# Nine transposed chunks of attention weights, moved through PSUM in three pieces of three instead of five and four

## The chip, the cores and the metric

The kernel runs on one core of a Trainium2 chip. The metric is the device time of one execution in microseconds, lower is better, and the number that is compared is the median of several executions.

## What is computed

A sparse attention, then two mixing blocks. All of it is float32.

```
q, k, v: (4 batches, 8 heads, 576 tokens, 64)
scores = q @ k^T / 8
mask   = scores >= 32nd largest score of the row
attn   = softmax of the scores under the mask          # 576 x 576 per head
x      = attn @ v, heads side by side                  # (4, 576, 512)

block 1: theta = x @ w_theta; zr, zi = x cos(theta), x sin(theta)
         u = x + w_tok_r @ zr + w_tok_i @ zi;  x = u + relu(u @ w_ch)
block 2: h = relu(x @ w_in), halves u and v; v normalised over its 512 channels
         out = (u * (w_spatial @ v + b_spatial)) @ w_out
```

## The kernel before

**The attention.** Two heads of a batch make a visit: 16 visits, each of nine tiles of 128 query rows by 576 keys (`NT = 9`; the ninth tile holds the last 64 rows of both heads). That makes 144 tiles, taken two at a time (`G = 2`): 72 pairs. What happens to a pair, function by function:

- `scores(n)`: four float32r matmuls into the PSUM tile `ps_s` (L449), and a copy by ScalarE (ACT) into the SBUF tile `x` (L453), for one tile of the pair.
- `topk(g)`: VectorE (DVE) finds the 32nd largest score of every row of both tiles. Max and min windows (L468, L469), MAX8 and MATCH_REPLACE8 (L472, L478, L481), then three small coefficients `cf` (L489 to L491, partly on ACT).
- `weigh(n)`: ACT makes a sign from the threshold (L500) and the exponential (L501), GpSimd (POOL) multiplies them into `sg` (the helper at L89, two pieces of 288 columns to a tile). `sg` holds both tiles of the pair side by side: 1152 columns of unnormalised weights, which is nine chunks of 128.
- `transpose(n)`: TensorE (PE) transposes the chunks into the PSUM tile `ps_t` (L511), and one ACT instruction copies them to the SBUF tile `ptb` (L512, a Relu, which also turns the negative products of masked keys to zero). The even tile's call takes chunks 0 to 4, the odd one's chunks 5 to 8. There is one `ps_t` of five chunks, 2560 bytes of each partition, which reaches over two banks. There are two `ptb`.
- `values(n)`: once for the pair, 9 to 20 matmuls of the transposed chunks with the values of `v` into `ps_v` (L522, L533, L536). Chunk 4, the one that holds the last columns of the even tile and the first of the odd one, goes first when both tiles have one row block each.

PSUM is full: `ps_s` has two banks, `ps_t` two, `ps_v` one, and `ps_m`, the rotating output of the mixing blocks, three.

**The mixing blocks.** They are generators (`block`, `front`, `middle`, `last`) that yield an estimated cost after each PSUM tile. Each product of two float32 operands is three float32r matmuls (`mm3`, L572 to L574). `advance(quota)` pulls them forward between the attention's steps, a fixed quota of estimated nanoseconds at a time. Batch b's blocks can begin when all of batch b's heads are done, so the first batch's attention (18 pairs) has next to no matrix work beside it, and the last batch's blocks run after the attention's end.

**What sets the order.** Every engine runs its instructions in a fixed order. A planner lays that order down when the kernel is built, out of priorities (`tc.high_priority`), of its own estimate of times, and of when buffers come free. `at(f, n)` calls a step under a raised priority. The calls of one pair stand in the loop as: `weigh` of both tiles, then for each tile `scores` of a later tile, `advance`, `transpose`, `advance`, and `values` at the end.

**Weights that are loaded early.** In the last batch, weights of three products go into attention buffers as these come free (`EXTRA`, `load_extra`): the last two chunks of the low half of `w_spatial` go into the two `ptb`.

Of the kernel before, what the change touches and what calls it, by code (L numbers as in the profile page):

```python
# [10 lines left out]
F32 = mybir.dt.float32  # L11
F32R = mybir.dt.float32r
I32 = mybir.dt.int32
AF = mybir.ActivationFunctionType
# [10 lines left out]
def sparse_attention_then_moe_kernel(  # L25
# [26 lines left out]
    G = 2  # L52
# [15 lines left out]
    att = ctx.enter_context(tc.tile_pool(name="att", bufs=2))  # L68
# [4 lines left out]
    psum = ctx.enter_context(tc.tile_pool(name="psum", bufs=1, space=bass.MemoryType.PSUM))  # L73

    act, dve, pe = nc.scalar, nc.vector, nc.tensor
# [21 lines left out]
    ident = const.tile([128, 128], F32, name="ident")  # L97
# [22 lines left out]
    for i in range(2):  # L120
        chunks = const.tile([128, 4, 3, D + 1], F32, name=f"vc{i}")
# [127 lines left out]
    def split_rest(exact):  # L249
# [9 lines left out]
        (B - 1, "ti"): [(f"{n}{s}", 2, 1) for n in ("q2", "k2") for s in range(2) for _ in range(2)],  # L259
        (B - 1, "ch"): [("x", 3, 2), ("x", 3, 2), ("sg", 2, 2), ("sg", 2, 2)],  # L260
        (B - 1, "sp"): [("kl0", 2, 1), ("kl0", 2, 1), ("kl1", 2, 1), ("kl1", 2, 1), ("raw", 2, 1), ("raw", 2, 1),
                        ("ptb", 2, 1), ("ptb", 2, 1)],
    }

    class Weights:
# [70 lines left out]
    def run(exact):  # L336
# [96 lines left out]
        X, SG, MX, PT = {}, {}, {}, {}  # L433
# [68 lines left out]
            pool.tensor_tensor(sg, x, sg, op=OP.mult)  # L502

        def transpose(n):
            x = SG[n // G].rearrange("p i n -> p (i n)")
            pt = psum.tile([128, 5, 128], F32, name="ps_t")
            ptb = att.tile([128, 5, 128], F32, name="ptb", bufs=2)
            k = (5, 4)[n % G]
            for c in range(k):
                lo = (c + 5 * (n % G)) * 128  # L510
                pe.transpose(pt[:, c, :], x[:, lo:lo + 128], ident)  # L511
            act.activation(ptb[:, 0:k], pt[:, 0:k], AF.Relu)  # L512
            PT[n] = ptb

        def values(n):

            pair = tiles[n - 1:n + 1]
            av = psum.tile([128, 3, D + 1], F32, name="ps_v")
            alone = any(t == 8 for _, _, _, t in pair)
            both = PT[n - 1][:, 4]  # L520
            if not alone:
                pe.matmul(av[:, 0:2], both, vaug[pair[0][0] % 2][1], start=True, stop=False)  # L522
            col = 0
            for i, (visit, b, j, t) in enumerate(pair):
                chunks, mixed, extra = vaug[visit % 2]
                pt = PT.pop(n - 1 + i)
                end = half[i]
                for s in range(2) if t == 8 else (t % 2,):
                    slot = 2 * s if t == 8 else s
                    q = half[s] if t == 8 else slice(0, 128)  # L530
                    o = av[0:64 if t == 8 else 128, col]
                    for c in range(4):
                        pe.matmul(o, pt[:, c, q], chunks[:, c, slot], start=alone and c == 0,  # L533
                                  stop=not alone and i == 1 and c == 3)
                    if alone:
                        pe.matmul(o, both[end, q], extra[end] if t == 8 and s == 1 else mixed[end, i], start=False,  # L536
                                  stop=True)
                    col += 1
            at = 0
            for i, (visit, b, j, t) in enumerate(pair):  # L540
                if t == 8:
                    act.activation(xr[0:64, 4], av[0:64, at:at + 2], AF.Copy)
                    at += 2
                elif alone or i == 0:
                    k = 1 if alone else 2
                    act.activation(xr.rearrange("p i s d -> p (i s) d")[:, t:t + k], av[:, at:at + k], AF.Copy)
                    at += 1

                if t == 8:
                    normalise(b, j, 3 if visit == NP - 1 else 0, 5)  # L550
                elif visit == NP - 1 and t % 2 and t < 7:
                    normalise(b, j, t // 2, t // 2 + 1)
# [3 lines left out]
        def normalise(b, j, lo, hi):  # L556
            if lo == 0:
                XN[b, j] = big.tile([128, 5, 2, D], F32, name="xn", bufs=6)
            xn = XN[b, j]
            i = slice(lo, hi)  # L560
            rs = tmp.tile([128, 5, 2], F32, name="rs")
            dve.tensor_scalar(rs[:, i], xr[:, i, :, D], 1e-9, None, op0=OP.add)
            dve.reciprocal(rs[:, i], rs[:, i])
            pool.tensor_tensor(xn[:, i], xr[:, i, :, 0:D], rs[:, i, :, None].to_broadcast([128, hi - lo, 2, D]),
                               op=OP.mult)
            if hi == 5:
                pool.tensor_tensor(xn[64:128, 4], xr[0:64, 4, :, 0:D],
                                   rs[0:64, 4, :, None].to_broadcast([64, 2, D]), op=OP.mult)
# [450 lines left out]
        for g in range(N // G + 2):  # L1019
            with tc.high_priority(offset=AHEAD):  # L1020
                if g < N // G:
                    topk(g)
                    with tc.issue_after(GATE[g]):
                        if g:
                            next(conv, None)
                        if g == SPLIT:
                            for _ in conv:
                                pass
            n0 = G * g
            for i in range(G):  # L1030
                step(n0 + i)
                at(weigh, n0 - G + i)
            q = FIRST_QUOTA if n0 < PER else QUOTA
            for i in range(G):
                at(scores, n0 + G + 1 + i)
                advance(q)
                at(transpose, n0 - G + i)
                advance(q)
                if i == G - 1:
                    at(values, n0 - G + i)  # L1040
# [52 lines left out]
```

## Time and profile before

| what | value |
| --- | --- |
| median of 3 executions | 989.75 us (989.65 to 991.41) |
| the profiled execution, its own time | 992.02 us |
| its span, first to last instruction | 990.2 us |
| PE busy | 867.8 us (88%) |
| PE weight loads (PEld) busy, beside PE | 797.5 us (81%) |
| DVE busy | 823.0 us (83%) |
| ACT busy | 638.0 us (64%) |
| POOL busy | 598.7 us (60%) |

The attention's last matmul starts at 838.0 us; the rest of the span is the last batch's mixing blocks. Busy times are sums over the span, which has stages with different limits, so a share of the whole says little about one stage. An idle time stands in front of an instruction, together with what ended it.

### The profile page before, as it was taken

The page shows a single profiled execution, that of the slowest core. Times are in us where ns is not written, and L with a number is a line of the kernel's source. Part 1 is how long each engine was busy: PE and PEld are TensorE (multiplying, and loading weights), DVE is VectorE, ACT ScalarE, POOL GpSimd, SP SyncE. Part 2 cuts the span into 40 slices and gives each one's busy share as a digit, 9 for nine tenths or more (in the row PEclk, how much of TensorE's full clock was granted, in tenths as well). Part 3 has the DMA queues.
Part 4 walks back from the last instruction along what each step waited for, and adds up shares of the span by engine and source line. Part 5 has one row for each costly group of instructions (what it writes and reads, how often), then busy time and mean ns, then how long its engine had stood idle before and what let it go on. Part 6 is the DMA issues. An engine that isn't in the chain of part 4 may idle for free.

```text
span 990.2 us, 18081 instructions
## 1 busy us (share of the span) xinstructions
PE 867.8 (88%) x5802; PEld 797.5 (81%) x5802; DVE 823.0 (83%) x2710; ACT 638.0 (64%) x1319; POOL 598.7 (60%) x753
## 2 busy tenths in 40 slices
PE   4657686678779799989999999999989999999997
PEld 2546575667669798888889998898889998889987
DVE  6999999999998897889999998999998981363552
ACT  5566676779858566877776777777966775350121
POOL 2798876686956755594767666676584564421030
PEclk9955556679779699999999999899999999999999
DMA  7797665545817633744362753552743554441221
GB/s 218 215 305 227 215 210 179 145 145 186 261 60 199 230 95 106 229 143 126 110 206 60 229 160 78 218 129 95 205 160 91 201 188 166 191 168 62 104 85 52
DMA packets 79395, 159.78 MB, mean 161 GB/s; under 512 B 36143, under 2 KB 40239, under 8 KB 71866
## 3 DMA queue, kind: packets, MB, share of 16 engines
q1 hardware_dynamic: 79290, 158.53, 50.5%
q8 instruction: 48, 0.79, 0.3%
q14 instruction: 57, 0.47, 0.2%
HBM read 108.63 MB, written 23.32 MB: 133 GB/s over the span
## 4 chain that ended last, share of the span: by engine, by line
PE 43%; DVE 26%; ACT 10%; DMA 9%; POOL 6%; issue 4%; SPq 2%; ACTq 0%; POOLq 0%; DVEq 0%
PE ps_m L574 9%; PE ps_m L572 9%; PE ps_m L573 9%; PE ps_v L533 7%; DVE mm L469 4%; PE ps_s L449 4%; PE ps_t L511 4%; DVE mm L481 4%; DVE mx L478 4%; DVE z L472 2%; DVE mm L468 2%; DMA raw<-in_q_dram 2%; DMA q<-hi 2%; ACT sg L500 1%; POOL sg L89 1%
## 5 line engine op out<-in xcount | busy, mean ns | idle before, releaser
L89 POOL TENSOR_TENSOR sg<-x,sg 128x288 f32<-128x288 f32 x288 | 238.5, 857 | 141.0 <-ACT x L501 94.2
L511 PE MATMUL ps_t<-ident,sg 128*128 128x128 f32 x648 | 140.9, 314 | 60.7 <-POOL sg L89 37.5
L533 PE MATMUL ps_v<-vc,ptb 128*128 128x65 f32 (+1 forms) x1280 | 183.5, 281 | 4.7 <-ACT ptb L512 4.7
L533 PEld LDWEIGHTS ps_v<-vc,ptb 128*128 128x128 f32 (+1 forms) x1280 | 174.7, 206 | 13.6 <-ACT ptb L512 6.7
L511 PEld LDWEIGHTS ps_t<-ident,sg 128*128 128x128 f32 x648 | 97.8, 171 | 77.6 <-POOL sg L89 51.2
L500 ACT ACTIVATE sg<-x,cf 128x576 f32<-128x576 f32 x144 | 103.8, 768 | 44.2 <-DVE cf L491 43.3
L478 DVE MAX8 mx<-mm 128x8 f32<-128x160 f32 x432 | 118.8, 312 | 0.0
L453 ACT ACTIVATE x<-ps_s 128x576 f32<-128x576 f32 x144 | 92.6, 643 | 35.9 <-PE ps_s L449 32.3
L512 ACT ACTIVATE ptb<-ps_t 128x640 f32<-128x640 f32 (+1 forms) x144 | 92.7, 644 | 29.8 <-PE ps_t L511 28.2
L501 ACT ACTIVATE x<-x,cf 128x576 f32<-128x576 f32 x144 | 107.9, 767 | 0.1
L449 PE MATMUL ps_s<-k,q 128*128 128x288 f32 x256 | 91.3, 368 | 16.2 <-DVE q L369 8.6
L572 PE MATMUL ps_m<-w_t,zah 128*128 128x288 f32 (+2 forms) x272 | 98.9, 364 | 6.6 <-DVE F L588 4.8
L574 PE MATMUL ps_m<-w_t,zal 128*128 128x288 f32 (+2 forms) x272 | 97.5, 360 | 0.6 <-POOL zal L89 0.5
L573 PE MATMUL ps_m<-w_t,zah 128*128 128x288 f32 (+2 forms) x272 | 96.7, 356 | 0.0
L472 DVE MAX8 z<-mm 128x8 f32<-128x312 f32 (+1 forms) x288 | 89.6, 372 | 2.0
L572 PE MATMUL ps_m<-w_t,zbh 128*128 128x288 f32 x288 | 85.7, 302 | 2.3 <-DMA w_t<-d_sph 1.0
L481 DVE MATCH_REPLACE8 mm<-mx,mm 128x160 f32<-128x160 f32 x288 | 86.8, 308 | 0.0
L573 PE MATMUL ps_m<-w_t,zbh 128*128 128x288 f32 x288 | 86.2, 303 | 0.0
L574 PE MATMUL ps_m<-w_t,zbl 128*128 128x288 f32 x288 | 84.9, 302 | 1.2 <-POOL zbl L89 1.2
L449 PE MATMUL ps_s<-kl,q 128*128 128x288 f32 x256 | 82.9, 334 | 0.0
L468 DVE TENSOR_TENSOR mm<-x 128x576 f32<-128x576 f32 x72 | 67.7, 941 | 17.5 <-ACT x L453 16.4
L89 POOL TENSOR_TENSOR raw<-raw,hi 128x288 fp32r<-128x288 f32 x60 | 56.2, 956 | 40.2 <-ACT hi L393 40.0
(174 smaller groups left out, 2438.9 us busy)
## 6 DMA issues: line engine op xcount, KB each, us to landing
k<-hi SPq DMA_DIRECT2D x60, 144.0 KB, 2.5
kl<-raw SPq DMA_DIRECT2D x60, 144.0 KB, 2.6
vc<-in_v_dram SPq DMA_DIRECT2D x48, 128.0 KB, 2.9
w_t<-d_trh SPq DMA_DIRECT2D x4, 1152.0 KB
w_t<-d_trl SPq DMA_DIRECT2D x4, 1152.0 KB
out_dram<-t SPq DMA_DIRECT2D x32, 144.0 KB, 2.5
raw<-in_q_dram SPq DMA_DIRECT2D x15, 288.0 KB, 3.0
q<-hi SPq DMA_DIRECT2D x30, 144.0 KB, 3.3
```

The costliest lines, as they stand in the source:

```text
L89: nc.gpsimd.tensor_tensor(out[:, lo:hi], a[:, lo:hi], b[:, lo:hi], op=op)
L449: pe.matmul(o, q, k[:, m], start=a == 0, stop=a == len(terms) - 1)
L472: dve.max(out=z[:, i, QUARTER + 8 * k:QUARTER + 8 * k + 8], in_=mm[:, i, losers])
L478: last = dve.max(out=top[i], in_=src[i])
L481: dve.match_replace(out=mr[i], in_to_replace=top[i], in_values=src[i], imm_value=NEG)
L500: act.activation(sg, x, AF.Sign, bias=cf[:, 2:3])
L501: act.activation(x, x, AF.Exp, bias=cf[:, 0:1], scale=0.125)
L511: pe.transpose(pt[:, c, :], x[:, lo:lo + 128], ident)
L533: pe.matmul(o, pt[:, c, q], chunks[:, c, slot], start=alone and c == 0, stop=not alone and i == 1 and c == 3)
L572: pe.matmul(out, ah, bh, start=first, stop=False)
L573: pe.matmul(out, ah, bl, start=False, stop=False)
L574: pe.matmul(out, al, bh, start=False, stop=last)
```

## The change

The nine chunks of a pair are taken in three pieces of three. Each piece has a PSUM tile of its own out of two (1536 bytes of each partition, so one bank each, two banks as before) and one of three `ptb`. The even tile's call takes piece 0 (chunks 0 to 2), the odd one's pieces 1 and 2. `values` reads chunks by their number out of a list. The two early loads into `ptb` become one, of both chunks, into the buffer `mm` of the top-k step.

```diff
@@ EXTRA
-                        ("ptb", 2, 1), ("ptb", 2, 1)],
+                        ("mm", 1, 2)],
@@ transpose
             x = SG[n // G].rearrange("p i n -> p (i n)")
-            pt = psum.tile([128, 5, 128], F32, name="ps_t")
-            ptb = att.tile([128, 5, 128], F32, name="ptb", bufs=2)
-            k = (5, 4)[n % G]
-            for c in range(k):
-                lo = (c + 5 * (n % G)) * 128
-                pe.transpose(pt[:, c, :], x[:, lo:lo + 128], ident)
-            act.activation(ptb[:, 0:k], pt[:, 0:k], AF.Relu)
-            PT[n] = ptb
+            for part in ((0,), (1, 2))[n % G]:
+                pt = psum.tile([128, 3, 128], F32, name="ps_t", bufs=2)
+                ptb = att.tile([128, 3, 128], F32, name="ptb", bufs=3)
+                for c in range(3):
+                    lo = (c + 3 * part) * 128
+                    pe.transpose(pt[:, c, :], x[:, lo:lo + 128], ident)
+                act.activation(ptb, pt, AF.Relu)
+                PT.setdefault(n // G, []).extend(ptb[:, c] for c in range(3))
@@ values
-            both = PT[n - 1][:, 4]
+            pts = PT.pop(n // G)
+            both = pts[4]
...
-                pt = PT.pop(n - 1 + i)
...
-                        pe.matmul(o, pt[:, c, q], chunks[:, c, slot], start=alone and c == 0,
+                        pe.matmul(o, pts[5 * i + c][:, q], chunks[:, c, slot], start=alone and c == 0,
```

## Rows read from the trace of the kernel before

**Rows 1.** The page's chain that ended last, by engine.
```profile
PE 43%; DVE 26%; ACT 10%; DMA 9%; POOL 6%; issue 4%; SPq 2%; ACTq 0%; POOLq 0%; DVEq 0%
```
**Rows 2.** Windows: stretch, length; busy us (count) of PE, PEld, DVE, ACT, POOL; PE clock; DMA.
```profile
50.00:250.00 200.00, 147.13 (x730) 125.24 (x731) 196.02 (x597) 145.94 (x294) 153.01 (x170) 0.63 0.64 201
250.00:350.00 100.00, 82.34 (x528) 76.33 (x527) 91.06 (x269) 67.78 (x142) 71.50 (x88) 0.82 0.58 182
350.00:838.00 488.00, 468.97 (x3467) 439.38 (x3465) 429.63 (x1554) 357.00 (x754) 313.40 (x397) 0.99 0.48 150
838.00:990.20 152.20, 143.20 (x981) 135.33 (x981) 65.36 (x157) 39.47 (x80) 37.36 (x47) 0.99 0.31 114
```
**Rows 3.** Waits of PE from 50 to 250 us: total, times, longest.
```profile
PE ps_t L511 <- POOL sg L89: 27.7, 15, 6.4
PE ps_t L511 <- ACT ptb L512: 9.6, 5, 3.7
PE ps_v L522 <- ACT ptb L512: 8.4, 7, 3.3
```
**Rows 4.** Waits of PE from 250 to 838 us.
```profile
PE ps_t L511 <- ACT ptb L512: 12.1, 6, 5.5
PE ps_t L511 <- POOL sg L89: 7.2, 8, 2.2
PE ps_s L449 <- ACT x L453: 2.7, 5, 1.4
```
**Rows 5.** Waits of PE from 350 to 838 us.
```profile
PE ps_t L511 <- ACT ptb L512: 4.4, 4, 2.4
PE ps_t L511 <- POOL sg L89: 2.6, 3, 1.7
```
**Rows 6.** Groups of instructions by form: busy us, mean ns, idle before and releasers.
```profile
L511 PE MATMUL ps_t<-ident,sg 128*128 128x128 f32 x648 | 140.9, 314 | 60.7 <-POOL sg L89 37.5 <-ACT ptb L512 21.6 <-POOL vt L588 1.2
L512 ACT ACTIVATE ptb<-ps_t 128x640 f32<-128x640 f32 x72 | 50.1, 696 | 13.0 <-PE ps_t L511 11.7 <-PE ps_v L533 1.0
L512 ACT ACTIVATE ptb<-ps_t 128x512 f32<-128x512 f32 x72 | 42.6, 591 | 16.8 <-PE ps_t L511 16.5
```
**Rows 7.** Timeline, PE from 200 to 260 us: start, length, instruction, [idle before].
```profile
213.12 0.61 PE L511 MATMUL ps_t<-ident,sg 128*128 128x128 f32 x4
217.20 0.47 PE L511 MATMUL ps_t<-ident,sg 128*128 128x128 f32 x1 [3.00 <-POOL sg L89]
218.46 0.80 PE L522 MATMUL ps_v<-vm,ptb 128*128 128x130 f32 x2 [0.79 <-ACT ptb L512]
```
**Rows 8.** Timeline, all engines, 281 to 297 us.
```profile
286.29 0.15 DVE L491 SCALAR_TENSOR_TENSOR cf<-cf,mx 128x2 f32<-128x2 f32 x1
286.48 1.44 ACT L500 ACTIVATE sg<-x,cf 128x576 f32<-128x576 f32 x2 [3.86 <-DVE cf L491]
287.83 0.68 ACT L512 ACTIVATE ptb<-ps_t 128x640 f32<-128x640 f32 x1
...
288.56 1.11 PE L511 MATMUL ps_t<-ident,sg 128*128 128x128 f32 x4 [5.48 <-ACT ptb L512]
...
296.03 0.65 ACT L453 ACTIVATE x<-ps_s 128x576 f32<-128x576 f32 x1 [5.07 <-PE ps_s L449]
```
**Rows 9.** Windows of 10 us, columns as in rows 2.
```profile
280.00:290.00 10.00, 4.52 (x32) 4.29 (x32) 9.90 (x24) 4.81 (x10) 6.45 (x9) 0.76 0.27 74
290.00:300.00 10.00, 10.00 (x62) 10.00 (x62) 7.49 (x28) 4.61 (x12) 3.99 (x6) 0.73 0.25 71
...
340.00:350.00 10.00, 10.00 (x72) 10.00 (x70) 9.90 (x35) 3.92 (x10) 3.25 (x4) 0.84 0.01 2
```
**Rows 10.** SP's queue around the attention's end, and the first PE wait afterwards.
```profile
838.02 0.80 SPq L284 DMA_DIRECT2D w_t<-d_spl  x2
840.04 0.32 SPq L284 DMA_DIRECT2D w_t<-d_thh  x1
840.48 0.35 SPq L284 DMA_DIRECT2D w_t<-d_thl  x1
```
**Rows 11.** Instructions on tile mm, 780 to 860 us: the last use of mm.
```profile
L478 DVE MAX8 mx<-mm x18: 261/314/322, 786.0 to 807.6; 128x8 f32<-128x160 f32 x18
```

## The prediction

> **What bounds the kernel now.** I read the chain of waits first, then busy times by stretch, then PE's waits by stretch. The chain is shared: 43% PE, 26% DVE, 10% ACT [rows 1], so no single engine's total gives the answer. The windows sort it into stages [rows 2]. From 50 to 250 us DVE is busy 196.0 of 200 us and PE 147.1, much of it at the lower clock (mean 0.63): the top-k step sets the pace and PE has 53 us to spare. From 350 to 838 us it is the other way: PE is busy 469.0 of 488 us at clock 0.99 and DVE 429.6, so a wait of PE there is worth up to its length. From 250 to 350 us both are short of full (PE 82.3, DVE 91.1 of 100): the mixing blocks begin, and each engine at times waits for the other. From 838 us on, 152.2 us, there is no attention, so the change has nothing to act on but a weight load. I therefore count what the change does to PE from 250 to 838 us, and nearly nothing of what it does before 250 us.
>
> Where do the transposes wait? PE's idle time before L511 is 60.7 us, of it 21.6 us for the copy out of `ps_t` and 37.5 us for POOL's product `sg` [rows 6]. The stages divide that unevenly. From 50 to 250 us it is 9.6 us for the copy and 27.7 us for POOL, and another 8.4 us in which `values` waits for a copy [rows 3]. From 250 to 838 us it is 12.1 us in 6 waits for the copy and 7.2 us for POOL [rows 4], of which 4.4 us in 4 waits and 2.6 us fall after 350 us [rows 5]. So 12.1 - 4.4 = 7.7 us in two waits lie between 250 and 350 us.
>
> The longer one can be read line by line [rows 8]. The second four transposes wait 5.48 us for the 640-column copy that must empty the only `ps_t`. That copy is itself late: ACT works in order, and ahead of the copy stand the two signs of the next pair, which waited 3.86 us for DVE's `cf`. When PE is through, it runs slowly: the granted clock is 0.73 on average in the following 10 us with PE busy throughout [rows 9]. The wait also reaches DVE: ACT's copy of the next scores had waited 5.07 us for PE [rows 8], and DVE, at 9.90 of 10 us before, falls to 7.49 [rows 9].
>
> **The change part by part.**
>
> *Transposes on PE.* 648 of the same size before and after, 9 to a pair. Cost 0.
>
> *Copies on ACT.* The two forms give the price: (696 - 591) / 128 columns = 0.82 ns a column, so 384 columns cost 591 - 128 x 0.82 = 486 ns [rows 6]. That form is not in the trace, so this is an estimate by a straight line. Three of them are 1458 ns against 696 + 591 = 1287: 171 ns more to a pair, 12.3 us more of ACT over 72 pairs. ACT is busy 357 of 488 us from 350 to 838 us [rows 2]; its spare quarter covers this, save where PE is waiting for ACT at that moment. From 250 to 838 us these are the 6 waits for the copy and 5 for ACT's copy of the scores [rows 4], so between 0 and 11 x 0.17 = 1.9 us. I take the middle, +1.0. Without that cover the whole 12.3 us would count, which is a rival below.
>
> *Two PSUM tiles instead of one.* The wait of the second transposes for the first copy goes. What is late next is the third piece, which needs the first piece's copy gone. Had that copy been stuck behind the signs as at 287.83 us [rows 8], PE would get three more transposes done, and then stand again. How much of a wait goes is not in the trace. The bounds are 0 (every copy is stuck as that one was) and all 12.1 us [rows 4]. A copy stuck for another reason than its own length gains little, but the first piece is ready sooner: it needs three chunks and these from the even tile alone, so its copy can be planned ahead of the signs. I take half, -6.0.
>
> The Trainium skill (Perfetto Trace Analysis, the section on optimizing tensor performance) says that independent groups should rotate through different PSUM banks, so that the copy out of one overlaps the next group's matmuls. By that rule the whole 12.1 us would go; the row of 287.83 us speaks for less, since that copy's own 0.68 us is the small part of the 5.48 us [rows 8].
>
> *The clock.* The mean 0.73 from 290 to 300 us and 0.84 from 340 to 350 us, PE busy throughout [rows 9], cost (1 - 0.73) x 10 + (1 - 0.84) x 10 = 4.3 us against full speed, right behind the two waits. With the waits halved I take half, -2.1; the bounds are 0 and 4.3.
>
> *The fifth chunk.* Before, the even tile's call held a chunk that ends in the odd tile, so its first copy waited for POOL's odd product: one transpose alone waits 3.00 us, and then `values` 0.79 us for the copy [rows 7]. Now the first piece needs the even tile only, and the last pieces' transposes can run while an earlier copy does. Both kinds of wait are mostly before 250 us, where DVE sets the pace [rows 2, 3]. Value there 0; if DVE were not ahead, 8.4 us of waits of `values` would be a bound [rows 3]. After 250 us a part of the 7.2 us for POOL [rows 4] may go; I count 0 and keep half, 3.6, for the range.
>
> *`ptb` by three.* Three buffers serve one pair, as two did, so the next pair's first copy still waits for this pair's first `values` matmuls. 0.
>
> *The load into `mm`.* One transfer instead of two; `mm` is last read at 807.6 us [rows 11], while the loads into `ptb` were issued at 838.0 us, followed on SP by the theta weights at 840.0 us [rows 10]. The new load can only go earlier, and no PE wait worth naming hangs on the old one. 0; if the theta weights did wait behind it, they would come up to 2 us sooner.
>
> *The order.* The planner lays all engines' orders down anew, and nothing in the trace says how. This is the largest unknown, and it carries the slower rival.
>
> Sum: -6.0 - 2.1 + 1.0 = -7.1 us. Against the profiled execution's own 992.02 us that is 984.9; the median of before is 989.75, 2.3 us lower, and I forecast against it: 982.6 us, 0.7% faster.
>
> **The rivals.**
>
> *More than forecast.* Two banks in rotation hide every copy, as the page's rule above would have it: all 12.1 us, all 4.3 us of clock and 3.6 us of the waits for POOL go, less 1.0: -19.0, about 971 us. For it: the two long waits lie on the chain between DVE and PE. Against it: they come from ACT's order more than from the number of buffers.
>
> *Nothing.* The waits only move to the third piece, because the copies are stuck behind signs that wait for DVE. Then the gain is 0 to 1.9 us, and the extra ACT work takes about 1 of it: 989 us. For it: the line at 287.83 us.
>
> *Slower, by the planned order.* With a tile always free, the planner can put the first three transposes, and later six in a row, on PE's queue as soon as it believes that the product is ready. POOL is late, PE works in order, and the mixing blocks' matmuls queue behind. From 50 to 250 us such a wait costs 27.7 / 15 = 1.85 us [rows 3]; from 350 to 838 us there are only 3 in 46 pairs [rows 5]. Four more (7.4 us) eat the forecast gain; with six more, 11.1 us, the time is 989.75 - 7.1 + 11.1 = 993.8 us. Against it: the transposes of single chunks could be planned as early before, chunk by chunk.
>
> *Slower, by ACT.* All of the 12.3 us lands on the chain (10% of it is ACT [rows 1]): 989.75 - 8.1 + 12.3 = 994 us. It decides from about two thirds of the pairs on (8.1 of 12.3). Against it: ACT's idle quarter.
>
> **How the numbers follow.** Forecast, a part of the waits gone (979 to 987.7 us): 0.42. More (below 979): 0.18. Nothing (within 0.2%, 987.8 to 991.7 us, about what a measurement of this kernel can tell from no change): 0.17. Slower by POOL and the order 0.18, by ACT 0.05. So faster 0.60, same 0.17, slower 0.23. The range takes in the whole-wait bound at 971 and the slower cases up to 994; about 0.06 lies below and 0.10 above. The forecast's own range is 979 to 987.7.
>
> **What the changed profile would show.** 216 copies at L512 of 384 columns near 486 ns, and ACT busy some 12 us more. PE's wait for `ptb` at L511 from 250 to 838 us near 6 us instead of 12.1, and `values` hardly waiting for copies before 250 us. The clock dips between 285 and 345 us shorter. PE's idle time from 350 to 838 us below 19 us, and the attention's end some 7 us before 838 us, with the tail behind it still near 152 us. The prediction is wrong if waits for POOL at L511 grow after 350 us, if DVE's waits for ACT's `x` grow, if the tail's length changes, or if the copies' price is not on the line.

## The result, and the profile after

The median went from 989.65 us (987.24 to 991.77, 7 runs) to 997.14 us (995.16 to 1003.71, 7 runs): ratio 1.0086, 95% interval 1.0062 to 1.0110. The change makes the kernel 0.9% slower; the forecast was 0.7% faster, and the measured time lies outside its range of 971 to 994 us. The profiled execution took 997.33 us, with a span of 995.5 us.

The lines of the changed kernel stand one or two further down: L511, L512, L522, L533 and L588 are now L512, L513, L524, L534 and L589.

The page of the changed kernel: busy time of the engines, and the chain that ended last.
```profile
PE 874.4 (88%) x5802; PEld 800.3 (80%) x5802; DVE 821.7 (83%) x2710; ACT 642.7 (65%) x1391; POOL 601.1 (60%) x753
...
PE 36%; DVE 28%; ACT 7%; DMA 5%; POOL 2%; issue 2%; SPq 0%; ACTq 0%; DVEq 0%; POOLq 0%
```
The shares of this chain add up to 80% only, so nothing is read from them here.

Windows of the changed kernel, columns as in [rows 2].
```profile
50.00:250.00 200.00, 147.11 (x730) 122.55 (x730) 195.04 (x590) 145.53 (x314) 152.95 (x167) 0.69 0.66 201
250.00:350.00 100.00, 86.16 (x566) 81.25 (x565) 92.83 (x290) 74.83 (x154) 75.73 (x96) 0.86 0.58 182
350.00:838.00 488.00, 464.91 (x3398) 434.66 (x3397) 425.50 (x1519) 351.71 (x784) 307.48 (x390) 0.98 0.47 147
838.00:995.00 157.00, 147.67 (x1012) 139.41 (x1010) 67.05 (x171) 42.26 (x86) 38.61 (x47) 1.00 0.32 120
```
Read PE's counts against [rows 2]: both kernels run the same 5802 matmuls. In both, 730 fall between 50 and 250 us. Between 250 and 350 us it is 566 against 528: here the trace has 38 matmuls more. From 350 to 838 us, called the full stretch from here on because PE is all but full in it, it is 3398 against 3467, 69 fewer; at that stretch's pace before, 488 / 3467 = 0.141 us each, this is an estimated 9.7 us (matmuls differ in size). It can be seen in the busy time (464.9 against 469.0 us, so 4.1 us more idle) and in the clock (0.98 against 0.99 of 488 us, some 5 us). At 838 us the changed kernel is 31 matmuls behind, and these make the end longer: 1012 matmuls from there against 981, and at the end's own pace, 157.0 / 1012 = 0.155 us, 31 of them are 4.8 of the 5.3 us by which the span grew.

PE's waits of the changed kernel from 250 to 350 us.
```profile
PE ps_m L573 <- DMA w_t<-d_chh: 3.7, 1, 3.7
PE ps_m L573 <- DVE t L589: 3.2, 1, 3.2
PE ps_m L573 <- ACT zbh L589: 2.6, 2, 1.7
PE ps_m L575 <- DVE zal L589: 2.1, 1, 2.1
PE ps_v L534 <- ACT ptb L513: 1.0, 1, 1.0
PE ps_t L512 <- POOL sg L89: 0.8, 1, 0.8
PE ps_t L512 <- ACT ptb L513: 0.4, 1, 0.4
```
The two waits of 7.6 us for the copy are gone. But PE's idle time in these 100 us fell only from 17.7 to 13.8 us, by 3.8: the mixing blocks' matmuls (`ps_m`) wait 11.6 us here, against 4.2 before, of which this was the largest:
```profile
PE ps_m L572 <- DVE F L588: 3.5, 1, 3.5
```
So about half of what the removed waits gave was spent again in the same stretch. And from 350 us on:
```profile
PE ps_s L449 <- ACT x L453: 12.1, 9, 4.0
PE ps_t L512 <- ACT ptb L513: 4.1, 3, 1.9
PE ps_t L512 <- POOL sg L89: 1.4, 2, 1.2
```
Before, the wait for the copy here was 4.4 us [rows 5]; it is hardly less with two tiles. New is 12.1 us at the scores, which must wait until ACT has emptied `ps_s`; before, that was 2.5 us here. The longest of the nine can be read in the timeline of the changed kernel: start, length, instruction, [idle before].
```profile
710.90 1.28 ACT L589 ACT_TABLE_LOAD   x1
712.20 2.19 ACT L589 ACTIVATE zbl<-zbl,upright 128x1024 f32<-128x1024 f32 x2
714.29 1.99 ACT L589 ACTIVATE zbh<-zbh 128x1024 f32<-128x1024 f32 x2
716.19 0.71 ACT L589 ACTIVATE zbh<-zbh,quarter 128x512 f32<-128x512 f32 x1
716.80 0.63 ACT L453 ACTIVATE x<-ps_s 128x576 f32<-128x576 f32 x1
717.33 0.27 ACT L547 ACTIVATE xr<-ps_v 128x130 f32<-128x130 f32 x1
...
717.48 0.40 PE L449 MATMUL ps_s<-k,q 128*128 128x288 f32 x1 [3.96 <-ACT x L453]
```
ACT's copy of the scores stands behind a mixing block's step, a table load (1.28 us) and five wide instructions from 710.9 to 716.8 us. PE, whose next instruction is the next scores, stands 3.96 us. Windows of the changed kernel show the granted clock around this wait and around another of the same kind.
```profile
655.00:665.00 10.00, 7.86 (x49) 7.54 (x48) 8.65 (x32) 6.10 (x13) 7.74 (x10) 0.83 0.36 90
710.00:730.00 20.00, 16.04 (x102) 15.60 (x101) 16.70 (x48) 15.14 (x29) 10.26 (x14) 0.83 0.13 43
```
Behind both waits the matmuls run slower for a while (288 columns take 0.44 us at 721.43 us, 0.29 us ahead of the wait). There are four such stretches after 350 us, at the lower of the clock's two levels (1.2 instead of 2.4 GHz), from 499.7, 561.2, 660.2 and 718.2 us; before, there are two. Three of the four begin in or just behind a wait at the scores; the one from 561.2 us begins behind a wait of 1.86 us for the copy.

The copies, and the transposes:
```profile
L512 PE MATMUL ps_t<-ident,sg 128*128 128x128 f32 x648 | 135.7, 311 | 42.4 <-POOL sg L89 32.6 <-ACT ptb L513 7.0 <-DVE mx L478 1.7
L513 ACT ACTIVATE ptb<-ps_t 128x384 f32<-128x384 f32 x216 | 102.9, 485 | 37.3 <-PE ps_t L512 35.8 <-PE ps_v L534 0.7
```

### The profile page after: what moved, and what is told of

The parts are those of the page before. It is cut to its first block, busy times and chain, and to the rows that moved or that the text cites. A ratio compares the mean times of both kernels' runs of the same rounds, so it can differ in the third digit from the quotient of the medians.

```text
span 995.5 us, 18200 instructions
## 1 busy us (share of the span) xinstructions
PE 874.4 (88%) x5802; PEld 800.3 (80%) x5802; DVE 821.7 (83%) x2710; ACT 642.7 (65%) x1391; POOL 601.1 (60%) x753
## 4 chain that ended last, share of the span: by engine, by line
PE 36%; DVE 28%; ACT 7%; DMA 5%; POOL 2%; issue 2%; SPq 0%; ACTq 0%; DVEq 0%; POOLq 0%
PE ps_m L573 9%; PE ps_m L575 9%; PE ps_m L574 8%; DVE mx L478 5%; DVE mm L481 5%; DVE mm L469 4%; PE ps_v L534 4%; DVE z L472 3%; DVE mm L468 3%; PE ps_t L512 3%; PE ps_s L449 2%; ACT sg L500 1%; DVE z L468 1%; DVE flags L485 1%; DVE F L589 1%
## 5 line engine op out<-in xcount | busy, mean ns | idle before, releaser
L89 POOL TENSOR_TENSOR sg<-x,sg 128x288 f32<-128x288 f32 x288 | 250.8, 900 | 134.2 <-issue 67.5
L534 PE MATMUL ps_v<-vc,ptb 128*128 128x65 f32 (+1 forms) x1280 | 179.6, 286 | 2.5 <-ACT ptb L513 2.5
L534 PEld LDWEIGHTS ps_v<-vc,ptb 128*128 128x128 f32 (+1 forms) x1280 | 170.2, 207 | 10.2 <-ACT ptb L513 3.9
L512 PE MATMUL ps_t<-ident,sg 128*128 128x128 f32 x648 | 135.7, 311 | 42.4 <-POOL sg L89 32.6
L512 PEld LDWEIGHTS ps_t<-ident,sg 128*128 128x128 f32 x648 | 88.8, 162 | 64.3 <-POOL sg L89 55.4
L513 ACT ACTIVATE ptb<-ps_t 128x384 f32<-128x384 f32 x216 | 102.9, 485 | 37.3 <-PE ps_t L512 35.8
L453 ACT ACTIVATE x<-ps_s 128x576 f32<-128x576 f32 x144 | 92.7, 644 | 28.1 <-PE ps_s L449 21.3
L449 PEld LDWEIGHTS ps_s<-k,q 128*128 128x128 f32 x256 | 56.0, 219 | 45.6 <-ACT x L453 37.3
L89 POOL TENSOR_TENSOR raw<-raw,hi 128x288 fp32r<-128x288 f32 x60 | 59.5, 1012 | 39.7 <-ACT hi L393 22.2
L573 PE MATMUL ps_m<-ph,w_t 128*128 128x288 f32 x256 | 79.1, 310 | 4.7 <-DMA w_t<-d_chh 4.5
```

Of the source, the lines that this page charges most:

```text
L89: nc.gpsimd.tensor_tensor(out[:, lo:hi], a[:, lo:hi], b[:, lo:hi], op=op)
L449: pe.matmul(o, q, k[:, m], start=a == 0, stop=a == len(terms) - 1)
L534: pe.matmul(o, pts[5 * i + c][:, q], chunks[:, c, slot], start=alone and c == 0, stop=not alone and i == 1 and c == 3)
L573: pe.matmul(out, ah, bh, start=first, stop=False)
```

## The experiments

The theories, in words: ACT's 72 more copies cost the time; the planned order that this change happens to get is an unlucky one; the split of the calls (three chunks early, six late) holds the pair back; the attention runs too far ahead of the mixing blocks; the next pair's transposes are put ahead of this pair's values and block PE; the second PSUM tile itself is what costs. All ratios are to the kernel before, run beside each. In the third column a comma parts the even tile's call from the odd one's, and a plus parts two pieces or copies of one call.

| run | `ps_t` | pieces or copies of a pair | else | median us | ratio [95%] | PE matmuls 250-350 | 350-800 | clock 350-800 |
| --- | --- | --- | --- | --- | --- | --- | --- | --- |
| before | 1 | 5, 4 | | 989.65 | 1 | 528 | 3202 | 0.99 |
| after | 2 | 3, 3+3 | | 997.14 | 1.0086 [1.0062, 1.0110] | 566 | 3158 | 0.98 |
| e1 | 1 | 5, 4 | load into `mm` | 990.05 | 1.0010 [0.9988, 1.0031] | 555 | 3186 | 0.98 |
| e2 | 1 | 3+2, 4 | | 978.66 | 0.9894 [0.9869, 0.9920] | 634 | 3209 | 0.99 |
| e3 | 1 | 3, 3+3 | | 1036.55 | 1.0474 [1.0442, 1.0506] | 527 | 3015 | 0.97 |
| e4 | 2 | 3, 3+3 | quota 2200 | 1001.73 | 1.0114 [1.0089, 1.0139] | 551 | 3126 | 0.97 |
| e5 | 1 | 5, 4 | quota 2020 | 987.92 | 0.9994 [0.9967, 1.0021] | 571 | 3205 | 0.99 |
| e6 | 2 | 3, 3+3 | quota 2020 | 996.11 | 1.0065 [1.0041, 1.0088] | 570 | 3140 | 0.97 |
| e7 | 2 | 3+2, 4 | | 993.43 | 1.0033 [1.0010, 1.0057] | 597 | 3130 | 0.97 |
| e8 | 2 | 3+3, 3 | | 991.46 | 1.0011 [0.9986, 1.0035] | 552 | 3189 | 0.99 |
| e9 | 2 | 3, 3+3 | ahead 250 | 997.46 | 1.0085 [1.0067, 1.0102] | 590 | 3159 | 0.97 |
| e10 | 1 | 3+2, 2+2 | | 989.89 | 0.9985 [0.9958, 1.0012] | 564 | 3200 | 0.99 |
| e11 | 1 | 4+1, 4 | | 982.57 | 0.9932 [0.9914, 0.9949] | 601 | 3172 | 0.98 |
| e12 | 2 | 3, 3+3 | transposes first | 1007.87 | 1.0167 [1.0140, 1.0193] | 564 | 3052 | 0.96 |
| e13 | 2 | 3, 3+3 | turn | 999.29 | 1.0111 [1.0067, 1.0155] | 549 | 3150 | 0.97 |
| e14 | 2 | 3+2, 4 | turn | 1001.41 | 1.0135 [1.0085, 1.0185] | 571 | 3104 | 0.97 |
| e15 | 1 | 5, 4 | turn | 987.18 | 0.9973 [0.9947, 1.0000] | 589 | 3184 | 0.97 |
| e16 | 1 | 3+2, 4 | turn | 1007.57 | 1.0201 [1.0140, 1.0263] | 565 | 3081 | 0.97 |
| e17 | 1 | 3+2, 4 | quota 2020 | 976.38 | 0.9862 [0.9822, 0.9902] | 612 | 3232 | 0.99 |
| e18 | 1 | 3+2, 4 | quota 1980 | 980.74 | 0.9900 [0.9858, 0.9942] | 593 | 3201 | 0.98 |

The last three columns are from one profiled execution each; those of e9 are from its quickest run (990.31 us, the others 994.7 to 999.7), so its row speaks for that run alone.

### The parts of the change one by one

**e1**, the kernel before with the new early load alone.
```diff
-                        ("ptb", 2, 1), ("ptb", 2, 1)],
+                        ("mm", 1, 2)],
```


> The kernel before, with nothing changed but the early load of the last w_spatial chunks, which goes into mm instead of the two ptb. Every theory: within 0.2% of before (988 to 992 us). If it is slower by more, the load is a part of the cause.


No difference: the load costs nothing, as the prediction had it. In its trace PE, ACT, DVE and POOL run the same instructions in the same order as before, to the last one. So it also shows how far two executions of one order differ:
```profile
250.00:350.00 100.00, 82.15 (x555) 77.26 (x554) 91.80 (x283) 69.86 (x143) 70.77 (x89) 0.88 0.57 179
```
That is 27 matmuls more than in the trace of before, and clock 0.88 for 0.82, with no gain in the median. The 38 matmuls and the clock of 0.86 of the changed kernel are hardly more than this. From 350 to 838 us the two differ by 20 matmuls (3447 and 3467), so the 69 that the change loses there stand out.

**e2**, the kernel before with one `ps_t` of five chunks, of which the even tile's call makes two copies: the number of copies of the changed kernel without its tiles.
```diff
-            act.activation(ptb[:, 0:k], pt[:, 0:k], AF.Relu)
+            for lo, hi in (((0, 3), (3, 5)), ((0, 4),))[n % G]:
+                act.activation(ptb[:, lo:hi], pt[:, lo:hi], AF.Relu)
```


> The kernel before, one ps_t and two ptb as they were, but the even tile's five chunks are copied by two instructions (three chunks and two), so ACT issues three copies a pair as after the change does. Theory A, the extra copy on ACT is what costs: most of the 7.5 us, 995 to 998 us. Theory B, the order that the planner makes out of two free PSUM tiles is what costs (the attention planned further ahead, PE waiting at the scores): the order of PE stays near that of before, so 988 to 992 us.


11 us faster than before. Its windows and, from 250 to 350 us, its PE waits at L511:
```profile
250.00:350.00 100.00, 88.62 (x634) 82.97 (x634) 95.88 (x317) 76.58 (x164) 76.37 (x95) 0.95 0.58 183
350.00:800.00 450.00, 431.60 (x3209) 406.14 (x3208) 416.46 (x1479) 335.65 (x748) 304.14 (x375) 0.99 0.50 155
```
```profile
PE ps_t L511 <- POOL sg L89: 0.8, 2, 0.5
PE ps_t L511 <- ACT ptb L513: 0.7, 1, 0.7
```
The 7.6 us of waits for the copy between 250 and 350 us go here too, with one tile. 106 more matmuls than before fall into this stretch at clock 0.95 (before 0.82), and at 0.141 us each that is 14.9 us, nearly all of the 15.1 us by which the profiled span is shorter (975.1); by e1's row some 27 of the 106 can be scatter. The full stretch is as before (3209 against 3202 from 350 to 800 us). So ACT's extra copies are not what makes the changed kernel slow.

What the split does not do is start a copy earlier. The even tile's two copies in e2's trace:
```profile
L513 ACT ACTIVATE ptb<-ps_t 128x384 f32<-128x384 f32 x72 | 34.7, 483 | 11.6 <-PE ps_t L511 10.1 <-PE ps_v L534 1.5
L513 ACT ACTIVATE ptb<-ps_t 128x256 f32<-128x256 f32 x72 | 27.4, 380 | 0.0
```
In none of the 72 pairs does the first one begin before the fifth transpose has ended, and in 71 the second one is ACT's next instruction, which is why no idle time stands before it. Two copies in a row do the work of one, 483 + 380 - 696 = 167 ns longer, and the planner lays another order around them: PE's parts from that of before at the 126th of its 5802 matmuls. So, as far as the trace shows, the gain is one of that order.

**e3**, the changed kernel with one three-chunk tile.
```diff
-                pt = psum.tile([128, 3, 128], F32, name="ps_t", bufs=2)
+                pt = psum.tile([128, 3, 128], F32, name="ps_t")
```


> The kernel after the change with one ps_t of three chunks instead of two: pieces and copies as after, no rotation. Theory A (copies cost): no better than after, and the waits for copies come back, 997 to 1010 us. Theory B (order): the attention is planned further back than in either kernel (2182 matmuls of the mixing blocks ahead of the last transposes, against 2024 before and 1865 after), PE waits more at the transposes and less at the scores; 985 to 998 us.


PE's waits over the whole run of e3 (the changed kernel: 7.0, 27.1, 32.6 and 3.4 us at the same places):
```profile
PE ps_t L512 <- ACT ptb L513: 40.2, 31, 5.6
PE ps_s L449 <- ACT x L453: 21.3, 22, 2.3
PE ps_t L512 <- POOL sg L89: 17.3, 10, 5.7
PE ps_v L524 <- ACT ptb L513: 10.4, 11, 3.2
```
Three pieces in one tile cost 46 us, and the second tile gives 39 of them back. The Trainium skill's rule of rotating banks (Perfetto Trace Analysis, the section on optimizing tensor performance) holds between these two kernels. But the pieces were made for it: one `ps_t` of two banks needs two round trips between PE and ACT for a pair, this one three.

### Is it the order that the planner happens to lay?

**e4, e5, e6**: the quota that the loop gives the mixing blocks per step, 2200 or 2020 for 2000; e5 is the kernel before, e4 and e6 the changed one.
```diff
-    FIRST_QUOTA, QUOTA = 2500, 2000
+    FIRST_QUOTA, QUOTA = 2500, 2020
```


> The kernel after the change with QUOTA 2200 instead of 2000: the same pieces, tiles and copies, another interleaving. If the loss belongs to the pieces themselves (A), 995 to 1000 us as after. If it belongs to one particular order (B), the time moves by more than 3 us, either way: 985 to 1005 us, and PE's waits at the scores with it.

> The kernel before with QUOTA 2020 instead of 2000, 1% more of the mixing blocks pulled at a time: a small disturbance of the planned order with nothing else changed. Theory B (the loss after the change is that of one particular order): even this moves the time by some 0.5% or more, 980 to 1000 us, outside 988 to 992. Theory C (the loss belongs to how three by three is called): 988 to 992 us, as before.

> The kernel after the change with QUOTA 2020. Theory B: another order, 980 to 1005 us, more than 3 us from 997. Theory C: 995 to 1000 us, as after.


A quota 1% larger gives another order in both kernels, and neither time moves beyond its interval. With 10% more the changed kernel's median is 4.6 us higher, but the intervals overlap. In the rows of e5 and e1 the stretch from 250 to 350 us holds 571 and 555 matmuls for 528, with no gain in time: a shift there alone proves little, the full stretch has to hold. The waits for the copy in this stretch are a matter of the order, too; in e5, with one tile and whole copies, they are 3.5 us for 7.6:
```profile
PE ps_t L511 <- ACT ptb L512: 3.5, 2, 2.0
```

**e9**: the changed kernel with a smaller raised priority for the attention's steps; **e12**: in the loop, `transpose` ahead of `scores`.
```diff
-    AHEAD, EDGE, URGENT, FRONT = 500, 1000, 1000, 2000
+    AHEAD, EDGE, URGENT, FRONT = 250, 1000, 1000, 2000
```
```diff
+                at(transpose, n0 - G + i)
+                advance(q)
                 at(scores, n0 + G + 1 + i)
-                advance(q)
-                at(transpose, n0 - G + i)
                 advance(q)
```


> The kernel after the change with the attention's raise of priority halved (AHEAD 250 instead of 500), so that the planner holds the attention back: 2001 matmuls of the mixing blocks stand ahead of the last transposes, as in before (2024) and unlike after (1865), and 24 groups of scores stand close behind another instead of 38 (before 20). The kernel before has the same order of PE at 250 as at 500. Theory D (two free tiles let the planner run the attention too far ahead): most of the loss goes, 984 to 992 us. If the lead is not the cause: 994 to 1000 us.

> The kernel after the change with the calls of transpose and scores swapped in the loop, so that the transposes are planned ahead of the next tile's scores (1944 matmuls of the mixing blocks ahead of the last transposes, 26 close groups of scores). Theory D: part of the loss goes, 986 to 995 us. If neither lead nor close scores matter: 994 to 1002 us.


e9 is as slow as the changed kernel, though it gives the attention's lead back (in its trace 2001 matmuls of the mixing blocks stand ahead of the last transposes, as expected, for 1865). PE's waits after 350 us in its profiled run:
```profile
PE ps_v L524 <- ACT xr L547: 5.6, 3, 3.6
PE ps_t L512 <- POOL sg L89: 4.5, 7, 0.9
PE ps_v L534 <- ACT ptb L513: 3.9, 1, 3.9
```
The wait at the scores has no line there, others have taken its place, and this was its quickest run. e6 has only 3.7 us of waits at the scores from 350 to 800 us, against 12.1, and is 996.11 us:
```profile
PE ps_s L449 <- ACT x L453: 3.7, 4, 1.5
```
So these waits are how the loss shows in one trace, not a cause that stays when the order moves. e12 is 10.7 us slower than the changed kernel; in its profiled run PE's waits for the copy from 350 to 800 us are 13.2 us in 4.

### The pieces, and the second tile by itself

**e7**: two tiles of one bank each, with exactly the pieces, copies and `ptb` of e2.
```diff
-            pt = psum.tile([128, 5, 128], F32, name="ps_t")
...
+            for first, last in (((0, 3), (3, 5)), ((0, 4),))[n % G]:
+                pt = psum.tile([128, 4, 128], F32, name="ps_t", bufs=2)
+                for c in range(first, last):
+                    lo = (c + 5 * (n % G)) * 128
+                    pe.transpose(pt[:, c - first, :], x[:, lo:lo + 128], ident)
+                act.activation(ptb[:, first:last], pt[:, 0:last - first], AF.Relu)
```
**e8**: the changed kernel with six chunks in the even tile's call and three in the odd one's.
```diff
-            for part in ((0,), (1, 2))[n % G]:
+            for part in ((0, 1), (2,))[n % G]:
```


> Two ps_t of one bank as after the change, but the pieces of the run with three copies (three and two chunks for the even tile, four for the odd one) and the two ptb of before. Theory C (three by three puts six transposes and two copies between the last scores and the values): the even call has five chunks again, so the gain of three copies stays, 976 to 984 us. Theory D (two free tiles let the planner put the attention too far ahead): 995 to 1002 us.

> The kernel after the change, but pieces 0 and 1 in the even tile's call and piece 2 in the odd one's: six chunks early and three late instead of three and six. Theory C: most of the loss goes, 978 to 990 us. Theory D: 994 to 1000 us. Theory B says only that it moves by more than 3 us.


Windows of e7, and its PE waits after 350 us:
```profile
250.00:350.00 100.00, 84.58 (x597) 79.80 (x596) 90.79 (x296) 71.17 (x151) 71.51 (x90) 0.91 0.55 175
350.00:800.00 450.00, 427.50 (x3130) 403.24 (x3130) 413.39 (x1480) 333.87 (x742) 295.24 (x369) 0.97 0.48 146
```
```profile
PE ps_t L511 <- ACT ptb L512: 10.1, 6, 6.5
PE ps_v L533 <- ACT ptb L512: 4.1, 3, 2.5
```
e7 against e2 is the cleanest pair: same transposes, same three copies, same `ptb`, and two one-bank tiles for one of two banks. It is 993.43 against 978.66 us, 15 us slower (by the two ratios, 1.0033 and 0.9894, 1.4%). By the Trainium skill's rule of rotating banks (same page and section) it should be the faster one; the measurement decides against it here. The overlap that the rule is after does come about: in 41 of e7's 72 pairs the first copy begins before the fifth transpose has ended, in e2 in none. The loss is once more mostly in the full stretch, 3130 matmuls against 3209 at clock 0.97 against 0.99 (and 597 against 634 from 250 to 350 us), and the wait for the copy, of which the second tile should leave less, is 10.1 us against 2.1 there. The two profiled executions lie 19 us apart, so these rows show somewhat more than the medians' 15 us.

e8 is 5.7 us quicker than the changed kernel, and their intervals do not touch; it cannot be told from before. Three early and six late, each with the order that the planner lays for it, is thus the larger part of the 7.5 us, and not of the distance to e2. It is one order of six and three; no neutral nudge was tried on it.

**e10**: four copies with one tile, and **e11**: copies of 4 + 1 and 4.
```diff
+            for lo, hi in (((0, 3), (3, 5)), ((0, 2), (2, 4)))[n % G]:
```
```diff
+            for lo, hi in (((0, 4), (4, 5)), ((0, 4),))[n % G]:
```


> The kernel before with four copies a pair (three and two chunks, two and two) instead of two. If the gain of three copies came from freeing the one tile in steps, the gain stays or grows a little, 974 to 981 us. If the third copy's gain was a chance of that order, back to 984 to 994 us. The extra ACT work by the straight line is 171 ns a copy, 24.6 us of ACT in all against before.

> The kernel before with three copies a pair, cut elsewhere: four chunks and one for the even tile (the one chunk is the one that waits for the odd tile's product), four for the odd tile. Shorter turn at the single tile: the last copy before the second transposes is one chunk, about 276 ns by the straight line instead of 696, so the gain stays, 974 to 984 us. Chance of an order: 984 to 994 us.


A split of the even tile's copy gains at both places where it was cut (e2, e11), and in e11, too, no first copy begins before the fifth transpose has ended. Where the odd tile's copy is split as well, the gain is gone (e10).

### The next pair's transposes

**e13 to e16**: the changed kernel, e7, before and e2, each with a rule for the planner that the first transposes of a pair come behind the last values matmul of the pair before. Counted in the traces over all 72 pairs, without the rule 1.8 to 1.9 transposes of the next pair stand ahead of it on average with two tiles (e7, after) and 1.2 to 1.4 with one (before, e2); with the rule, none. The diff is that of e15.
```diff
+            with ExitStack() as turn:
+                if n % G == 0 and "values" in TURN_OF:
+                    turn.enter_context(tc.issue_after(TURN_OF["values"]))
+                for c in range(k):
...
-                        pe.matmul(o, pt[:, c, q], chunks[:, c, slot], start=alone and c == 0,
-                                  stop=not alone and i == 1 and c == 3)
+                        TURN_OF["values"] = pe.matmul(o, pt[:, c, q], chunks[:, c, slot], start=alone and c == 0,
+                                                      stop=not alone and i == 1 and c == 3).ins
```


> The kernel after the change with one rule of order more: piece 0's transposes of a pair are issued after the last pair's last chunk matmul of values. Transposes of the next pair ahead of it fall from 2.3 a pair to 0.2 (before: 1.5). Theory E (two free tiles let the next pair's transposes stand on PE's queue ahead of this pair's values, and PE works in order): the loss goes, 978 to 991 us. Otherwise 995 to 1003 us.

> Two one-bank tiles with pieces of three, two and four, with the same rule. Theory E: towards the one-tile kernel with these pieces (979), so 975 to 986 us. Otherwise 991 to 998 us, as without the rule (993).

> The kernel before with the same rule. One tile already keeps most transposes behind the values (1.5 a pair ahead, to 0.2). Theory E: little to gain, 982 to 991 us. If the rule helps or hurts by itself, whatever the tiles, it moves here as much as in the two-tile kernels.

> The fastest so far (one tile, three copies, 979 us) with the same rule. Theory E: 973 to 982 us, little change. If the rule costs by itself, 983 us or more.


The theory falls: without early transposes neither two-tile kernel is faster; the changed one is 2 us slower, within the intervals, and e7 8 us. Before doesn't mind the rule. In its trace with the rule (e15) no transpose waits for a copy from 250 to 350 us, with one tile and whole copies, and the largest waits there are now:
```profile
PE ps_m L577 <- DVE F L593: 8.1, 2, 4.8
PE ps_t L516 <- POOL sg L89: 7.9, 3, 6.6
```
So the 7.6 us can go and bring no gain that is clear of noise. e2 loses 29 us by the rule: against its own trace, e16 has 54 matmuls less from 50 to 250 us, 69 from 250 to 350 and 128 from 350 to 800. PE's waits of e16 from 250 to 350 us, where e2 has 0.7 us for the copies:
```profile
PE ps_v L539 <- ACT ptb L518: 7.3, 3, 4.9
PE ps_t L516 <- ACT ptb L518: 4.0, 3, 1.9
```

### The quicker kernel

**e17, e18**: e2 with quota 2020 and 1980, as in e5.


> One tile, three copies (979 us at QUOTA 2000), with QUOTA 2020. A gain of the finer copies themselves: 975 to 984 us. The chance of one order: 984 to 1000 us.

> The same with QUOTA 1980. A gain of the finer copies themselves: 975 to 984 us. The chance of one order: 984 to 1000 us.


The gain of e2 holds over three planned orders: 976.38, 978.66 and 980.74 us, 1.0 to 1.4% below before. Against the changed kernel that is 16 to 21 us. The stretch from 250 to 350 us does not carry this alone: e18 has 593 matmuls there, and e15 has 589 with no gain clear of noise.

## Why the prediction was wrong

*Transposes, copies, the load, `ptb`.* Right. The copy of 384 columns takes 485 ns (forecast 486); all copies together are 102.9 us against 92.7 [rows 6], 10.2 us more (forecast 12.3). ACT's whole busy time grew by 4.7 us, not 12. The load costs nothing (e1). That ACT has room for the copies is shown by e2, e17 and e18, which make as many; the rival "slower, by ACT" falls.

*Two PSUM tiles instead of one (-6.0).* The size was near: 12.1 us of waits for the copy from 250 to 838 us became 0.4 + 4.1 = 4.5, so 7.6 went. But nearly all of it lies between 250 and 350 us, next to nothing in the full stretch (4.4 to 4.1), and half of it came back there at the mixing blocks' matmuls. Nor does it need a second tile: e2 removes it, and in e5 and e15 it is 3.5 and 0 us with whole copies and the time of before. I put the wait down to the one tile being occupied; it was the place of the copy in ACT's order, as [rows 8] had shown.

*The clock (-2.1).* It rose from 0.82 to 0.86 between 250 and 350 us, as forecast, but e1, with the order of before, has 0.88 there, so this shows no gain. After 350 us there are four stretches at the lower level where there had been two.

*The order (0).* This is the step that failed. I gave it no value, because nothing in the trace says how the planner will lay it, and summed the removed waits as if everything else stayed. Between 350 and 838 us, where PE is all but full, the new order loses 69 matmuls, an estimated 9.7 us, more than the 38 gained before. The rival of the slower side had this sign and place but the wrong line: not POOL at L511 after 350 us (2.6 us before, 1.4 after) but ACT's in-order queue in front of the scores' copy (2.5 to 12.1 us), in this trace. Nine two-tile kernels (after, e4, e6 to e9, e12 to e14) took 991 to 1008 us, and none was faster than before. Eight of them do 3052 to 3159 matmuls from 350 to 800 us (e8 3189), where the kernels with one tile of five chunks do 3172 to 3232, but for e16 with its rule. The groups lie close (one order alone gave 3202 and 3186, before and e1), and e8 stands with the other one. So the loss is no chance draw of one order (e4, e6 and e9 keep it), and it goes with the second tile in eight of nine; that the tile is its cause is not shown.

*The fifth chunk (0).* As forecast: the waits of `values` at L522 for a copy from 50 to 250 us fell from 8.4 [rows 3] to 1.8 us, and both kernels do 730 matmuls there.

*What was to be seen.* PE's idle time from 350 to 838 us is 23.1 us, not below 19. The attention's last matmul starts at 813.5 us, 24.5 us earlier and not 7, and what follows takes 182 us instead of 152: the attention ran ahead of the mixing blocks, whose matmuls were left for the end. An earlier end of one stage is worth nothing if it was paid with another's work. Nor is it the loss itself: e2's attention ends earlier still (its last matmul starts at 810.8 us) and e2 is faster, and e9 takes the lead back and is as slow. Waits of DVE for `x` did not grow (16.4 to 11.6 us at L468).

*What stays open.* Why the second tile costs 15 us at equal pieces (e7 against e2): early transposes, ACT's copies, the attention's lead and the waits at the scores were each tried or moved, and none carries it alone. Six late transposes are worth some 5.7 us by the medians (e8, one order). Why the order that comes with a split of the even tile's copy fills the stretch from 250 to 350 us, though it starts no copy earlier, and why the rule of e16 takes that away while before doesn't mind it, is also open. Two tiles of five chunks, which would leave before's calls whole, were not tried, since PSUM is full.

## What to carry to other kernels

A wait that is taken away counts only if the engine's next instructions don't wait in its place: compare the idle time of the whole stretch, not only the wait, check the fullest engine's count of instructions stage by stage, and ask what its in-order queue, and that of the engine which empties its PSUM, will hold next. Making pieces smaller so that buffers can rotate adds round trips; an edit that only splits a copy is cheaper to try, but look in the trace whether the first part starts any earlier (here it never did) before the gain is put down to it. Where a planner lays the order, run the change with a neutral nudge of it (here a quota 1% larger) before a difference of 1% is believed.

## What the runs showed of the hardware and the order

ACT's copies out of PSUM lie on one line: 273 ns for 128 columns (e11), 380 for 256 (e2), 485 for 384 (after), 589 for 512 (e2), 696 for 640 [rows 6], so some 170 ns and 0.82 ns a column. A fourth instruction to a pair is 72 x 0.17 = 12 us more of ACT, and e10 is 11 us slower than e2, though ACT is busy only 65% of the span and the third one had come with a gain; whether it is the instruction or the order that it brings was not told apart. A single rule for the order moved e2 by 29 us, and a 1% quota nothing beyond the intervals. One profiled execution can be 7 us from the median of its kernel (e9), and two of one order can differ by 27 matmuls in 100 us (before and e1), so the rows of one are not the kernel's time.
